# Ten normalisations moved from VectorE to ScalarE in the first of four layers, with the order of work written anew

## The chip, the core and the metric

The kernel runs on one core of a Trainium2 chip. The core has five engines that run side by side, each through its own queue in order: TensorE (PE, with its weight loads shown apart as PEld), VectorE (DVE), ScalarE (ACT), GpSimd (POOL) and SyncE (SP), which issues most of the DMA transfers. The engines wait for each other by semaphores. The metric is the device time of one execution in microseconds (us).

## The reference, cut to what matters

The input x has 2048 rows of 512 in bfloat16. Four layers follow each other, each with a residual: A, B, A, B. Every layer first normalises its rows, without a learned scale.

```python
def _layernorm(x, axis=-1, eps=1e-5):
    m = jnp.mean(x, axis=axis, keepdims=True)
    v = jnp.var(x, axis=axis, keepdims=True)
    return (x - m) / jnp.sqrt(v + eps)

x = x + _A_ref(_layernorm(x, axis=-1), A_wqkv, A_wo)   # linear attention
x = x + _B_ref(_layernorm(x, axis=-1), B_wqkv, B_wo)   # sliding window of 256
x = x + _A_ref(_layernorm(x, axis=-1), A_wqkv, A_wo)
x = x + _B_ref(_layernorm(x, axis=-1), B_wqkv, B_wo)
```

Layer A has 32 heads of 16. It makes q, k and v, applies phi(t) = t + 1 for t > 0 and exp(t) otherwise (plus 1e-6) to q and k, sums k times v and k over all rows, and each q row reads these sums: o = (phi(q) kv) / (phi(q) z). Layer B is softmax attention with the same heads, where a row sees itself and the 255 rows before it. Both end with a multiplication by wo.

## The kernel before, in words

The 2048 rows are 16 tiles of 128 rows, on the 128 partitions. x stays in SBUF (`xres`) and is updated in place by every layer; weights are loaded once.

The class `Plan` writes every piece of work as an operation with a name, the engines that may run it, what it reads and writes, and its PSUM banks. `Graph.add` makes the dependencies. The order is not found at run time: `place` (lines 88 to 120) unpacks a byte table, `TABLE`, that holds the order of all operations, the engine of each (for those that have a choice) and the PSUM bank of each tile. `synchronise` (line 123) turns dependencies into semaphore waits, and `play` (line 912) emits each engine's queue in the table's order. So each engine works strictly in the table's order, and an instruction that waits holds up all that is behind it on its engine. `FILL` (line 857, read at line 945) lists after which of PE's first operations how many matmuls without use are put in. They, and nine more before the first operation (line 921), only keep PE at work until data is there.

Normalisation of a tile is the function `norm` (lines 326 to 335): DVE makes the row statistics (`stats`, L330, and `aggr`, L331, which leaves mean and variance in `mv`), POOL adds the small constant (`eps`, L332, into `ve`) and raises to the power of minus one half (`pow`, L333, into `rs`), and DVE applies it, (x - mean) * rs (`xn`, L334). Then the tile is transposed (`transpose`, line 337). In the first layer PE transposes tiles 0 to 4 (L346) and ACT or DVE copies the result out of PSUM (`Te`, L353); tiles 5 to 15 go by a DMA transpose that SP issues (L340).

The first layer's front half is `layer_a_keys` (lines 428 to 471). For each tile t it normalises, makes k on PE (L369), takes phi of it and multiplies the normalised tile with phi(k) into four PSUM banks that run on over all tiles (operations `g`, two a tile, L444). q (L383) is made for each tile too, two halves a tile. phi (line 388) is three instructions: exp on ACT (`E`, L392), min and add on DVE (`E1`, L393), and a max on DVE (`phi`, L394). After tile 15 the four banks go to SBUF (`ge`, L358), are multiplied by wv (`gv`, L458), and `barrier` (line 473) forms the sums, M = kv wo and the denominators. From then on `middle` (line 733) runs layer A's output, layer B tile by tile and the next layer's front in one pipeline, twice. In it the exponentials of scores (L609, L641), masks (`mk`, L615; `mf`, for the far edge of the window, L649 on POOL or L650 on DVE), and evictions from PSUM (`bqe`, `bke`, `bve`, `ve`: queries, keys and values) share DVE, ACT and POOL.

Loads: SP issues all first loads in the order of line 261, and from the eighth on each waits for an earlier one. The last of the first burst is 1 MB of B's weights (`pb<-in_B_wqkv`), and the DMA transposes of the first layer follow it in SP's queue. While the first layer runs POOL also makes constants and masks and re-orders B's weights (`wBp`, L316).

Of the kernel before, what the change touches and what calls it, by code (L numbers as in the profile page):

```python
# [8 lines left out]
ACT = mybir.ActivationFunctionType  # L9
# [203 lines left out]
class Plan:  # L213
# [112 lines left out]
    def norm(self, t, key, xn_slot, out, wr, by_pe):  # L326

        K = self
        xn, name = (lambda: K.vA[:, t, :], ("vA", t)) if xn_slot is None else (lambda: K.xn[:, xn_slot, :], ("xn", xn_slot))
        self.on("DVE", "stats", lambda e: e.bn_stats(K.stats[:, t, :], K.xres[:, t, :]), key, dve(512), rd=[("xres", t)], wr=[("stats", t)])  # L330
        self.on("DVE", "aggr", lambda e: e.bn_aggr(K.mv[:, t, :], K.stats[:, t, :]), key + 0.01, (66, 150), rd=[("stats", t)], wr=[("mv", t)])  # L331
        self.on("POOL", "eps", lambda e: e.tensor_scalar(K.ve[:, t, :], K.mv[:, t, 1:2], LN_EPS, None, op0=ALU.add), key + 0.02, (300, 330), rd=[("mv", t)], wr=[("ve", t)])  # L332
        self.pow = self.on("POOL", "pow", lambda e: e.tensor_tensor(K.rs[:, t, :], K.ve[:, t, :], K.negh[:], ALU.pow), key + 0.03, (640, 690), rd=[("ve", t), ("negh",)], wr=[("rs", t)])  # L333
        self.on("DVE", "xn", lambda e: e.tensor_scalar(xn(), K.xres[:, t, :], K.mv[:, t, 0:1], K.rs[:, t, :], op0=ALU.subtract, op1=ALU.mult), key + 0.04, dve(512, "ptr"), rd=[("xres", t), ("mv", t), ("rs", t)], wr=[name])  # L334
        self.transpose("T", xn, out, [name], wr, key + 0.05, by_pe)
# [92 lines left out]
    def layer_a_keys(self, ph, base):  # L428
# [5 lines left out]
        for t in range(T):  # L434
            k = 100 * ph + t
            self.norm(t, k - 0.5, None, lambda t=t: K.XQ[:, :, t * P:(t + 1) * P], [("XQ", t)], t < self.par["pe_first1"])
# [359 lines left out]
    r"c-rk(1Jq?nlFo<>WR`8)wr$(CZQHhO+qP|2wQYCpd+)ER>6z)7?d|Q|b9PU~|G&KV2EL5=B3_<%jfrF;8#GZ(6a&T@Hqi{3=q9BR6T`$bsZ44U",  # L796
    r"%cL=}O&pWf#5L)Rnmi_+NpJF+_@=$dVDg##CZkDUI+#JGqse3{nyIFk>0}C+X(qENXq-uCN}435kntv|8Emqc#wMKEX_}bCX1SSenwo4TndxkX",
    r"m>Fh;X=b{ZT_(IaZL*uLCWk3yikrgbuIXlSn&zgv*=_EbnI@6xVa}LbW|qlnhMJY;7gNr(Fsn>YGt8VdtIcq8-?TKn%tvO88DYws(xxPwGb7C?",
    r"6B&w_*=CO!ZO)rH=2w&4d~7b52d0l1W9FK@rnebuJ~1!NJ~PjJYSx;EX1-ZxN|<q`j7bXX%_FnGj5h{0n9s~YlMFVRYUXou(PW29X1^(GqQGU7",
    r"!W=N0%@vaz4w_OB6|S1crZhY;Dd3O+Xbgu<4TG@BJT*tmQIis)!58M4Nd>u0eRJJBHx*13^QCEJu9+9+D^tmof#_i2YZC)<Kuz<FA!uzFaza^n",  # L800
    r"$FwoIpd1J^fp1M)lN(ZlLLHL_(m*>?*QAB-jDrZKDWrqSCOyQ2dL|b1HMLD_=x5?Ud8lRjo48N`JWPa&kQWA+d=MWhK~Xc%#Do0M$Yg{JP#Gqe",
    r"MP{)n01Zq*SYir6LsJ+gnn`A<X$F&EnW+jbpbFH5de9MS!(_9?R5w#h9jI!ynodw3wwVUd5E{XD(;1GL=FkOpn3m8Ux<M;w3+<pQw1(rR4RnAT",
    r"=7i}1lVJ*UhovwTmcdDL2ByKg<}56SZE({}hf`(-yl1w<Ot@uMz${n^=U_Ihg73|0m;*bYC%kVKz#7;IYhfWAhudZm?1Emf8&1F;SPXOFB-}Cc",
    r"Afo9FKbXBRAI?J`*attFjnEG^!8-WBEP<cQX1D--;Ua{CQ*a4BH0vQ8{%peIWe5-b;R;m12rvK+!3H=C5g`I@fk$uzDq<vf0!Lv#RKf#r8XiML",
    r"{1C3fRyYVB!$)uzjzJ`>jFIskM8Rut1*771xDTH~G`xzR!&A5cpFkD73D@v5cnDST8C1htFbN;P3#g8h@eX_e@o@@1hZL9quVX5Vj_*JXjDZO;",
    r"B__d`*bozAGQ5F}a4O!0FJT}w#-un62f@4W6*R@^7z<}$226yhF*e@BjF=p6;d_t?;$SAs4DZ8COoLy;Ec^hnKwA6;vfyAyhjlP3WX1IO6V%0Q",
    r"P!qFZW^9J_uogDK7ML9uV{Kf5&G9yN!ljr4?_g)li7oMG$c0_-7s!pRups^lv#~YK!I$t9+u&UM7M`KOt{4vizlXbs_#ETnJ^T(VcEkHP4+(qV",
    r"4=^7KVO#8udGJRljP)@eR)Zqg0INe@EQ;;0J=TB)xB_cJ0w{((u{f^64p;ygYk}ZO?1%}W1S+n<)z}O3<610<z0qMQT!#;^5B9}Gum#uSVBCO-",
    r"VJmLKB(M=ZF2jeo376w$e1t<_JC??wPzIyfvKZYChY?T?ci=E60y{B=9fIX?DDJ|dFbs>qhZxh=wjbectYc%@;TYTQ!H+SH9f8GRFV?jq@mm~)",
    r"`*4AcYrn@55YH~O`|&%hXWzx-_9%XW@8Kdl8sEo$xY$0mi*Skk0Y}18`wrH(&ujxb3I<?*Y-q<|3LD>kfXi%3`y~#<WB4^bw}bFFCa_=O2|R#}",  # L810
    r"?5B7TM?+(~+<t?fVM2QdGuY4ZG5&}zY({$+U*Jjn2{YLz_ywl1@7SMlEWT?O;xCxij>98pZF74HGu!ca8gtn9Y&zS*PQcW5BA&sVHkD0p6WRA|",
    r"V%yT@vU%)T%wm(+y!ISswfSsEo6R<{*=;AA+cvfNE!k$av+ZixcC!Vn*e<raJ&$TH;IG)jUc`bnnSF_uu#LTpZLP6|th0S>Ve4%>8_t%r8*P6J",
    r"c9ZRA2U@i4ZFt+$4zerk0K3`tvV-k5o7DEUrR;V)#73~CZ6CYCma)6+P}{+lwY%*a`++TIciOeKyxn6f*dlhF9cGK#y>_J?ZY$bi_K+Q6E7?`{",
    r"h>d7V*wr?Y9cK^QG4Q1=ZpT7o`<2~lCqOFt+HSF_X*{&D<KURBY+KtX_JmDCRcusS)sD2s?T5CSU2m(~kL(6J+NP!Pc7jbuAKRlgJ)N@??I@dp",
    r"+EWM0NEhrR`-#m&pW2i5yxnIf+p%_vooe^nj`W%R$zHNw*aP;IJ!pTno#?dv#eQec*ex{8cBb#`S-X|G(69Eg%}rzMHu}NlAxn8F8%?)NUFk=g",
    r"ox0IWOLWoZpl__wb~4nR9POaYw3C25Wg(<p^tlx(Kw0UE{ni$ut2P|Xum$OwooS2Ebvw(3r=oPj&bBvg1e#-S*<w_IBGNY$i3(Fi>P^L|58bwv",
    r"s0`h)ed${&OC{(#ia{l*GL@t6X(;ue;gpZcQ&0MVO3{y$pLSCf8b&`+Y3fB)X(UynyS6%wrV(_{)}@~*CXJ$46q)YZ*ffB0QWSb%2hu}(l=e_m",
    r"8brq^4o#)wRF4MJ7@9_LDH_G2TvVSP+4wY_hENT9Y!gsTicSe>u5Cc`Y%MxK4XHmJr1`cEO{9L*hz`+Mnnb_Q6FZI?(+rwSP3RPjr@b_RPSX@h",
    r"MEmFrC8qs!j*?JQnn`Er0yU$gG>ekadAdcj3HT(<q1%Lfkrq*H61IGYu95Nyx<Sq9E;(*N*Xa^nrj~S*!gDKHOjjr(U!^6~nj&yyUP||98Aav$",
    r"w4Czs3W~xHXeGtwhm@Zq@pFp9tLRrMz%MB-&!yF5I62Luc$|WwaU1eHpHfnMK0<9N0WYMpe3;tNIZnur=mjkx=Ew97CE{?rhTf$ow3dk9qxX3o",  # L820
    r"CFc(~I<Kdc{60OS4RoGUa18!{I&n<?kUr$%9E(5V#9We}(#M>HOK@RM%}Kc+cjjbVgwyaf?!wo(D3{{${1I)W3j8q@<4shWEAnP4!-Y5%-{8tz",
    r"mM?H6uFB>3BH!dHe2IJWE$+kB_!GL#pHg4$&T08G>c>6#bNYnS@fXyCKjrjXoj>Cm+>0~taPG?e`Ewr0HTer3z#}*#*Wye(m<MtL&dguZARfx2",
    r"_$$i7mw5<(O<8#<U*Y9k!w%zRT${V`3a)9davdJcb$JXo<gr}KHsXa`pU3fH9?xI$B5ustxE^QcCY*ztGRQ`5#$WMf&dJSr32$PQuek-U<=p%Y",
    r"uj7`yh4b)w{+1_jUf#eHITugj?|3VJ&y#r@ujC*2N1no~cq(t_X}p75@oH|*cX&Fl;TilB-{pI}ldUwD`@D-E@NVA2E#x8Z<<|U&_i-DZ$1}MD",
    r"&*#UypWE^QCOOE5cow(g!#tax@DYB>3z+37pW<UYhv)KfKF!a#BR}U8e3D=A8GeV~<@fk!ZYFspkNm>L<X0{t;ib4lkfQRE3rPtv5>Z47O96=_",
    r"`6RNGl>DMnN(zdT($Z2|Nf~J^V`ZGglr~aUdP^T^E90e|#FF;XSC&W==^*{2qb!w9;w7r|mkBaJVoNs}D9fa~Oq9+tNG3@S2`7VPvUHK2GDPA?",
    r"Ihi6|rI!qqxDri<NqLzn!)1g_laW$EmP<t$CDCQNtdJ_QQpU(CsVp;OmduvXGE*wae5oo6WR9$sW3o{0$Xq!gG32f+lC5%F?#VpaCEMh_ES5bI",
    r"MYqcuiK@Hhft-?u5=}plM{-)CYZ)!8XC#K6lusq5K9&z9mX^~e@|k=t@g%m!m-3oecF0GvRuV`Yt)Tm4uT<1^@`db|N}5nM$a>i+N#uZ>m8bHt",
    r"B$8*6R1V5Uc`lb^lN^#{a#*fNa@i~|<Q+L8Tja7Fl`rL8`9$LCR}xRJ%KLIouE}|cuV2fLazPU4Mfq7OYf`-~-$*k3NfK&uttN@|S4pYW#b_1%",
    r"R=$(8@{7Ebbn?BtCpDz5{vhcEG?k{%dYVB}Yeu;tH>JL&QPEq1npjoSs@1AW>NK6QR@3mBUTdh=>RMAXXf~~-Q#FT9(~KHUhv;<8u8nl4HqlI)",  # L830
    r"Q-^70ZLGsJmqySmnny=yR*k45b(E%%+!{$!%4jX5sU)wC(d?31a!6!NBl)z57S`IDUz=)9X{H6Vffm(F(n1?*X2~T5^|mC@+|pdzX&oJ_?X`op",
# [182 lines left out]
```

## Time and profile before

| | us |
|---|---|
| median of 8 runs (lowest, highest) | 431.86 (430.44, 432.97) |
| the profiled execution | 431.93 |
| its span, first to last instruction | 430.2 |
| PE busy (share of the span) | 392.8 (91%) |
| DVE busy | 355.7 (83%) |
| ACT busy | 347.7 (81%) |
| POOL busy | 127.9 (30%) |

How to read it: the page gives one execution. A line such as "L334 DVE TENSOR_SCALAR vp<-xres,mv,rs" names the source line, the engine, the operation and the tensors written and read; "x14" is a count. In a timeline the first number is the start in us from the beginning of the span and the second the duration; several instructions in a row can be one line. What stands in brackets is the time the engine was idle just before, and what ended that idleness. Matmuls are pipelined, so their ends are modelled, and a matmul's duration is longer than the pace at which they follow each other. In a table by stretches each engine has its busy time and, in brackets, its instructions. The granted clock is the share of full speed at which TensorE was allowed to run. `vp` is the tensor that holds the normalised tiles of the first layer in its first half and phi(k) in its second.

### The profile page before, as it was taken

The page shows a single profiled execution, that of the slowest core. Times are in us where ns is not written, and L with a number is a line of the kernel's source. Part 1 is how long each engine was busy: PE and PEld are TensorE (multiplying, and loading weights), DVE is VectorE, ACT ScalarE, POOL GpSimd, SP SyncE. Part 2 cuts the span into 40 slices and gives each one's busy share as a digit, 9 for nine tenths or more (in the row PEclk, how much of TensorE's full clock was granted, in tenths as well). Part 3 has the DMA queues.
Part 4 walks back from the last instruction along what each step waited for, and adds up shares of the span by engine and source line. Part 5 has one row for each costly group of instructions (what it writes and reads, how often), then busy time and mean ns, then how long its engine had stood idle before and what let it go on. Part 6 is the DMA issues. An engine that isn't in the chain of part 4 may idle for free.

```text
span 430.2 us, 17035 instructions
## 1 busy us (share of the span) xinstructions
PE 392.8 (91%) x7471; PEld 258.0 (60%) x7548; DVE 355.7 (83%) x796; ACT 347.7 (81%) x433; POOL 127.9 (30%) x223
## 2 busy tenths in 40 slices
PE   8799999998899999999999999999798979998775
PEld 3445676766465566565566768576556746665544
DVE  5998899998998799898887789988797688866464
ACT  2433547998999999999997255999998989999992
POOL 4789222101240242121302303213044324242000
PEclk9999999999999999999999999999999989999889
DMA  7933015442152533552323001461443522553321
GB/s 240 274 74 87 2 33 168 116 101 65 39 124 51 108 98 74 113 99 67 81 46 56 15 2 50 110 119 42 113 76 89 117 77 68 106 136 99 79 53 50
DMA packets 66978, 37.81 MB, mean 88 GB/s; under 512 B 48248, under 2 KB 61816, under 8 KB 66904
## 3 DMA queue, kind: packets, MB, share of 16 engines
q1 hardware_dynamic: 66176, 34.75, 35.1%
q0 software_dynamic: 720, 1.97, 1.3%
q8 instruction: 59, 0.97, 1.0%
q14 instruction: 15, 0.12, 0.1%
q10 hardware_dynamic: 8, 0.00, 0.0%
HBM read 6.29 MB, written 2.10 MB: 20 GB/s over the span
## 4 chain that ended last, share of the span: by engine, by line
PE 40%; ACT 38%; DVE 14%; issue 4%; DMA 2%; POOL 1%; SPq 0%; POOLq 0%; ACTq 0%
ACT pb L609 24%; PE ps L369 14%; PE ps L383 11%; ACT pb L641 7%; PE ps L674 6%; PE ps L599 4%; ACT vp L609 4%; DVE vp L394 2%; DVE XQ L526 2%; DVE stats L330 2%; ACT tE L392 2%; DVE tE L393 1%; DMA xres<-in_A_x_dram 1%; DMA XQ<-vp 1%; DVE vp L334 1%
## 5 line engine op out<-in xcount | busy, mean ns | idle before, releaser
L609 ACT ACTIVATE pb<-ps 128x1024 bf16<-128x1024 f32 (+2 forms) x224 | 207.7, 1036 | 7.8 <-PE ps L599 6.7
L674 PEld LDWEIGHTS ps<-vB,pb 128*128 128x128 bf16 x2560 | 78.1, 96 | 13.3 <-DVE pb L615 2.9
L674 PE MATMUL ps<-vB,pb 128*128 128x34 bf16 x2560 | 83.8, 178 | 2.0 <-DVE pb L615 0.6
L392 ACT ACTIVATE tE<-ps 128x512 bf16<-128x512 f32 x64 | 39.0, 613 | 40.9 <-PE ps L369 18.7
L383 PE MATMUL ps<-xT,wBp 128*128 128x128 bf16 x1024 | 69.6, 220 | 2.3 <-DVE pb L650 1.5
L332 POOL TENSOR_SCALAR ve<-mv 128x1 f32<-128x1 f32 x64 | 16.5, 258 | 175.6 <-DVE mv L331 173.8
L383 PEld LDWEIGHTS ps<-xT,wBp 128*128 128x128 bf16 x1024 | 58.9, 98 | 14.9 <-issue 3.8
L615 DVE TENSOR_TENSOR pb<-pb,tri 128x512 bf16<-128x512 bf16 x112 | 47.7, 433 | 11.9 <-ACT pb L609 11.2
L599 PE MATMUL ps<-XQ,kB 32*128 32x256 bf16 (+2 forms) x1024 | 50.3, 271 | 6.8 <-ACT pb L609 3.7
L641 ACT ACTIVATE pb<-ps 128x1024 bf16<-128x1024 f32 x50 | 49.7, 1071 | 1.4 <-PE ps L632 1.4
L369 PE MATMUL ps<-wA,XQ 128*128 128x512 bf16 x177 | 46.2, 380 | 4.0 <-DVE vp L394 0.7
L537 DVE TENSOR_TENSOR xres<-ps,xres 128x512 bf16<-128x512 f32 x63 | 43.0, 684 | 8.3 <-PE ps L369 7.3
L649 POOL TENSOR_SCALAR_AFFINE_SELECT pb<-pb 128x1024 bf16<-128x1024 bf16 x30 | 35.2, 1174 | 38.1 <-ACT pb L641 36.9
L330 DVE BATCH_NORM_STATS2 stats<-xres 128x6 f32<-128x512 bf16 x64 | 43.1, 680 | 3.0 <-DMA xres<-in_A_x_dram 2.4
L333 POOL TENSOR_TENSOR rs<-ve,negh 128x1 f32<-128x1 f32 x64 | 37.1, 579 | 5.3
L383 PE MATMUL ps<-XQ,wA 128*128 128x128 bf16 x512 | 36.1, 219 | 0.4 <-DVE vp L394 0.2
L369 PE MATMUL ps<-M,XQ 128*128 128x512 bf16 x115 | 32.4, 387 | 4.0 <-ACT vp L609 1.2
L599 PEld LDWEIGHTS ps<-XQ,kB 32*128 32x128 bf16 x1024 | 15.4, 93 | 34.1 <-ACT pb L609 15.1
L383 PEld LDWEIGHTS ps<-XQ,wA 128*128 128x128 bf16 x512 | 30.6, 98 | 7.6 <-DVE vp L394 1.2
L369 PE MATMUL ps<-wBv,xT 128*128 128x512 bf16 x106 | 31.1, 385 | 2.7 <-issue 0.8
L369 PE MATMUL ps<-wBo,oT 128*128 128x512 bf16 x104 | 29.4, 387 | 4.5 <-DVE vp L555 1.2
L685 DVE RECIPROCAL rc<-ps 128x16 f32<-128x16 f32 x64 | 16.1, 251 | 16.3 <-PE ps L674 15.8
(109 smaller groups left out, 540.6 us busy)
## 6 DMA issues: line engine op xcount, KB each, us to landing
vB<-vS SPq DMA_DIRECT2D x64, 136.0 KB, 2.6
kB<-vp SPq DMA_DIRECT2D x64, 128.0 KB, 2.2
out_dram<-xres POOLq DMA_DIRECT2D x15, 128.0 KB, 2.7
wA<-in_A_wqkv_dram SPq DMA_DIRECT2D x3, 512.0 KB, 6.3
xres<-in_A_x_dram SPq DMA_DIRECT2D x2, 512.0 KB, 5.0
pb<-in_B_wqkv_dram SPq DMA_DIRECT2D x1, 1024.0 KB, 8.9
xres<-in_A_x_dram SPq DMA_DIRECT2D x3, 256.0 KB, 5.3
wAo<-in_A_wo_dram SPq DMA_DIRECT2D x1, 512.0 KB, 7.6
```

The source lines that it names most:

```text
L330: self.on("DVE", "stats", lambda e: e.bn_stats(K.stats[:, t, :], K.xres[:, t, :]), key, dve(512), rd=[("xres", t)], wr=[("stats", t)])
L333: self.pow = self.on("POOL", "pow", lambda e: e.tensor_tensor(K.rs[:, t, :], K.ve[:, t, :], K.negh[:], ALU.pow), key + 0.03, (640, 690), r ...
L369: m = e.matmul(K.ps(ps), lhs(c), rhs(c), start=c == 0, stop=c == 3)
L383: m = e.matmul(K.ps(ps)[:, f * P:(f + 1) * P], w(c, f), xT(c), start=c == 0, stop=c == 3)
L392: self.on("ACT", "E", lambda e: e.activation(K.tE[:, s, :], K.ps(ps), ACT.Exp, bias=0.0), key, act(512), wr=[("tE", s)], ps=[ps])
L537: self.on("DVE", "res", lambda e: e.tensor_tensor(K.xres[:, t, :], K.ps(po), K.xres[:, t, :], ALU.add), key, dve(512), rd=[("xres", t)], w ...
L599: m = e.matmul(K.ps(ps[gq])[:, ns * i:ns * i + ns], K.kB[rows, j % 4, 2 * f + b, :, :], K.XQ[rows, f, q:q + ns], start=True, stop=True, ti ...
L609: return e.activation(out(2 * h, 2, ns), i, ACT.Exp, bias=0.0, scale=0.25)
L615: return e.tensor_tensor(x, x, K.tri[:, 0, :].unsqueeze(1).unsqueeze(1).to_broadcast([P, 4, n, 64]), ALU.mult)
L641: return e.activation(far(h), i, ACT.Exp, bias=0.0, scale=0.25)
L649: return e.affine_select(out=x, in_=x, compare_op=ALU.is_ge, fill=0.0, base=-2, pattern=[[0, 16], [-2, 64]], channel_multiplier=1)
L674: m = e.matmul(K.ps(ps)[:, 34 * u:34 * u + 34], K.P((b // 2) % rp)[:, gq, f, o:o + P], K.vB[:, (b // 2) % 4, b % 2, r, :], start=i == 0, s ...
```

## The change: what it does

In the first layer, for tiles 2 to 11, `xn` is no longer one DVE instruction (x - mean) * rs but an ACT instruction, Identity(rs * x + b), with one scale and one bias per row. The bias b = -mean * rs is a new operation, `nb`, which may run on POOL or DVE and writes over `ve`. Tiles 0, 1 and 12 to 15 of the first layer and all later layers keep `xn` on DVE. Besides, `eps` may now run on DVE in all layers.

```diff
-        self.on("POOL", "eps", lambda e: e.tensor_scalar(K.ve[:, t, :], K.mv[:, t, 1:2], LN_EPS, None, op0=ALU.add), key + 0.02, (300, 330), rd=[("mv", t)], wr=[("ve", t)])
+        small = {"POOL": (300, 330), "DVE": (66, 150)}
+        self.g.add("eps", small, lambda e, eng: e.tensor_scalar(K.ve[:, t, :], K.mv[:, t, 1:2], LN_EPS, None, op0=ALU.add), key + 0.02, rd=[("mv", t)], wr=[("ve", t)])
         self.pow = self.on("POOL", "pow", lambda e: e.tensor_tensor(K.rs[:, t, :], K.ve[:, t, :], K.negh[:], ALU.pow), key + 0.03, (640, 690), rd=[("ve", t), ("negh",)], wr=[("rs", t)])
-        self.on("DVE", "xn", lambda e: e.tensor_scalar(xn(), K.xres[:, t, :], K.mv[:, t, 0:1], K.rs[:, t, :], op0=ALU.subtract, op1=ALU.mult), ...
+        if by_act:
+            self.g.add("nb", small, lambda e, eng: e.tensor_scalar(K.ve[:, t, :], K.mv[:, t, 0:1], K.rs[:, t, :], -1.0, op0=ALU.mult, op1=ALU.mult), key + 0.03, rd=[("mv", t), ("rs", t)], wr=[("ve", t)])
+            self.on("ACT", "xn", lambda e: e.activation(xn(), K.xres[:, t, :], ACT.Identity, bias=K.ve[:, t, :], scale=K.rs[:, t, :]), key + 0.04, act(512), rd=[("xres", t), ("ve", t), ("rs", t)], wr=[name])
+        else:
+            self.on("DVE", "xn", ...
...
-            self.norm(t, k - 0.5, None, ..., [("XQ", t)], t < self.par["pe_first1"])
+            self.norm(t, k - 0.5, None, ..., [("XQ", t)], t < self.par["pe_first1"], 2 <= t < 12)
...
-FILL, SPARE = {1: 2, 4: 1, 6: 6}, 6
+FILL, SPARE = {1: 1, 6: 5, 7: 1}, 6
```

`TABLE` is replaced as a whole. Unpacked, the two tables compare so:

- Operations: PE 858 in both, SP 228 in both, DVE 795 before and 827 after, ACT 432 and 443, POOL 219 and 186.
- `eps` is on DVE for 13 of the first layer's 16 tiles and for 19 of the 48 later ones. Nine of the ten `nb` are on DVE, that of tile 7 on POOL.
- Later engine choices: 12 `mf` go from POOL to DVE and 10 from DVE to POOL. `bve` 1, 3 and 11 and `bqe` 10 and 13 go from DVE to ACT, `bke` 11 and `bve` 12 from ACT to DVE, all in the second layer; `ve` 9 and 14 go to DVE at its end. One `ge`, one `bke` and one `Te` go to DVE; one `oTe`, one `recb` and one `Te` go to ACT.
- Order: of PE's 858 operations 248 stand elsewhere among the others, by at most 12 places; SP's first 27 are as before. In the first layer the transpose of tile 3 now stands ahead of the k of tile 2, and one more `g` stands ahead of the k of tile 5. ACT's queue begins Te 1, E 0, E 2, xn 2, xn 3, Te 2, Te 3, E 4, xn 5, xn 4, E 6, Te 4, xn 6, E 3, E 8, xn 8.

## The prediction

> **What bounds the kernel now.** The time per stretch comes first, because the change works in the first 60 us of a 430 us span. The columns are the stretch, its length, and the busy time of PE, weight loads, DVE, ACT and POOL, then the granted clock, the DMA share and GB/s.
>
> ```profile
> 12.00:25.00 13.00, 10.78 (x64) 4.76 (x64) 12.95 (x35) 5.26 (x9) 9.90 (x24) 1.00 0.85 227
> 25.00:37.00 12.00, 11.78 (x94) 6.03 (x94) 11.37 (x26) 3.47 (x6) 10.61 (x19) 1.00 0.33 67
> 37.00:43.00 6.00, 5.64 (x52) 3.08 (x53) 4.57 (x9) 2.84 (x5) 5.49 (x9) 1.00 0.47 110
> 43.00:54.00 11.00, 10.50 (x158) 7.45 (x159) 9.79 (x18) 6.03 (x12) 3.10 (x5) 1.00 0.01 1
> ```
>
> From 12 to 25 us DVE never rests (12.95 of 13.00) and ACT is 40% busy: there is room to move work to ACT. PE is idle for 2.2 us there, but for only 0.2 of the next 12. So DVE is late early, and from 25 us on PE is the bound. A gain can only be PE's lost slots, and the timeline of PE alone shows those that are marked:
>
> ```profile
> 14.02 0.40 PE L346 MATMUL ps<-ident,vp 128*128 128x128 bf16 x4 [0.27 <-DVE vp L334]
> ...
> 18.02 0.40 PE L346 MATMUL ps<-ident,vp 128*128 128x128 bf16 x4 [0.30 <-DVE vp L334]
> ...
> 19.59 1.02 PE L369 MATMUL ps<-wA,XQ 128*128 128x512 bf16 x4 [0.74 <-DVE vp L394]
> 21.34 1.04 PE L369 MATMUL ps<-wA,XQ 128*128 128x512 bf16 x3 [0.74 <-DMA XQ<-vp]
> ...
> 39.29 1.07 PE L383 MATMUL ps<-XQ,wA 128*128 128x128 bf16 x16 [0.21 <-DVE vp L394]
> ```
>
> Two waits are for xn of tiles 3 and 4 (L334, what the change moves), one for a phi (L394, queued behind xn on DVE), and one for the first DMA transpose, tile 5. Each costs about 0.17 more than marked, since the last matmul's modelled end (0.38 for 512 columns, while eight in a row take 1.89, so 0.216 each) hides the drain. Together: 0.44 + 0.47 + 0.91 + 0.91 = 2.73 up to 21.34, and 0.38 at 39.29.
>
> Then the DMA answers, for that fourth wait:
>
> ```profile
> pb<-in_B_wqkv_dram SPq DMA_DIRECT2D x1, 1024.0 KB, 8.9
> XQ<-vp SPq DMA_TRANSPOSE x11, 2.5
> DMA to landing us min/median/max: 2.4/2.5/4.7
> ```
>
> The last weight load of the burst is issued at 11.89 and takes 8.9, so it lands at 20.8. Tile 5's transpose, issued at 16.61, needs 4.7 where the usual one needs 2.5, and lands at 21.3, half a us after that load. It stood behind the load.
>
> **The change part by part.** Durations are those of the profiled execution: 430.2 span, 431.93 in all, so 1.73 outside it; it stands 0.07 above the median of the eight runs, 431.86.
>
> xn off DVE. These rows give the prices:
>
> ```profile
> 24.98 0.41 DVE L334 TENSOR_SCALAR vp<-xres,mv,rs 128x512 bf16<-128x512 bf16 x1
> 25.31 0.17 DVE L331 BATCH_NORM_AGGREGATE mv<-stats 128x2 f32<-128x6 f32 x1
> 25.40 0.66 DVE L394 SCALAR_TENSOR_TENSOR vp<-ps,tE 128x512 bf16<-128x512 f32 x1
> 14.45 0.60 ACT L353 ACTIVATE XQ<-ps 128x512 bf16<-128x512 bf16 x1 [0.44 <-PE ps L346]
> ```
>
> The ten xn of tiles 2 to 11 are the third to the twelfth of their row: 0.40, 0.64, 0.38, 1.28 for two, 0.39, 0.40, 0.41, 0.41 and 0.41, in all 4.72; less the 0.09 by which the next one overlaps each, DVE gets back 3.8.
>
> Onto DVE in layer one: nine of the ten biases and 13 of the 16 eps, by the new table. No row has that form on DVE; aggregate (L331) is the nearest in size, 0.09 from start to start and 0.17 alone. The bounds are 22 x 0.09 = 2.0 and 22 x 0.17 = 3.7. I take 2.2, because the new order puts other work between most dependent pairs. DVE nets 1.6 (between 0.1 and 1.8).
>
> On ACT: ten of 0.60 by the copy of equal size (L353); the dearest 128x512 eviction, L554, is 0.77. That is 6.0 to 7.7, beside 5.26 of 13 busy and 3.47 of the next 12: cover that is there. Each xn adds a wait to ACT's queue (bias, scale), and behind it stand the evictions Te and exps E, which DVE's E1 and PE's next bank wait for. Walking the new queue, xn 3 ends near 11.8 (13.96 before), xn 5 near 14.7 (16.6), xn 4 near 15.5 (18.0). Te 2 falls behind xn 3: near 12.3 against 11.8, so tile 2's k starts some 0.3 later; tile 3's transpose, now ahead of it, no longer stops PE afterwards.
>
> [...]
>
> A second function on ACT beside Exp and Copy: the trace has one table load (1.28 at 2.02) for 433 instructions of two kinds. If Identity needed another, up to 18 switches of 1.28, 23 us; taken as zero, because Copy already shares Exp's.
>
> PE, the sum. The first three waits (1.82) go. What is late next is tile 5's transpose: SP would issue it near 14.7 instead of 16.61, but it still stands behind the load that lands at 20.8. So PE's fourth wait grows from 0.9 to nearly 2. Tile 5's k starts near 20.9 (0.44 earlier) with one more g group (0.43) done ahead of it by the new PE order: 0.87 at that point. From there PE streamed to the end of the stage but for 0.25 near 35.2, 0.38 at 39.29 and 0.22 near 41.0; DVE now runs over 1 us ahead, so I take 0.7 of these 0.85. Stage: -1.55, bounds -0.3 (fourth wait only, all else taken by dearer small instructions) and -2.7 (every marked wait up to 21.34).
>
> POOL loses 13 x 0.258 here and gains one bias; its 9.9 of 13 busy falls, and wBp, which it makes by 40 us, is wanted at 59.7: worth nothing. FILL goes from nine warming matmuls to seven, in gaps where PE waits for tile 2 (10.73): nothing, unless the granted clock, which is full in all these stretches, falls late; if it came after k 0 and k 1 they would take 1.7 longer, of which the gap before tile 2 hides 0.5: at most 1.2.
>
> Later layers. DVE gets 19 eps at 0.09 to 0.17 (1.7 to 3.2), and two more far masks on balance (12 from POOL, 10 to it) at 0.71 (L650): 1.4. DVE is 0.6 to 0.95 busy there and ACT up to 0.99, so DVE's queue hides most. ACT takes five evictions between 65 and 190 us and gives two, then gives two at the second layer's end: near zero over all, plus or minus 1.8 where they lie. The other orders differ by swaps of neighbours: of PE's 858 items 248 shift, none by over 12. I charge 0.25 for all of this; a gain from swaps is as possible as a loss, bounds -1 and +2.
>
> Sum: -0.87 - 0.7 + 0.25 = -1.3. Against 431.93 that is 430.6.
>
> **The rivals.** *Same:* the transpose wait is all that matters early. DVE's saving is used up by the 22 small instructions at 0.17 (net 0.1), the later waits stay, and only 0.44 is won, less 0.25: 431.7. For it: DVE stays the fullest engine. Against: three of the four waits are for things queued behind xn.
>
> *Larger gain:* the transpose lands early too. For it: the load is nearly through by 18.5. Then all 2.73, and 0.85 later, less the charge 0.25, is 3.3; with the two ends half met, 2.5: 429.4. Against: the landing half a us after the load.
>
> *Slower:* ACT in layer two. Five evictions come to it (bve 1, 3 and 11, bqe 10 and 13: three of 0.675 by L358 into vS and two of 0.605 by L358 into XQ, 3.2), two leave (bke 11, bve 12: 0.77 + 0.675). Net +1.8 between 65 and 190 us, where ACT is 78 to 98% busy; with a stage gain of only 0.3: 433.4. It decides once ACT's loss there exceeds the stage's gain, that is, if ACT paces PE already from 65 us, not only from 110. For it: 19.45 and 19.61 of 20 busy at 110 and 150 us. Against: bve 1 and 3 lie at 65 to 86, where ACT still has gaps, and leave +0.44 behind them.
>
> *Not what it says:* Identity reloads tables, 431.9 + 23 = 455.
>
> **How the numbers follow.** Main 0.46, same 0.19, larger 0.14, slower 0.19, reload 0.02. About 0.2% (0.86 us) is what a measurement of this kernel can tell from none, so faster is below 431.0 and slower above 432.7. The main case's own range is 429.9 to 431.3; five sixths of it is below 431.0. Faster: 0.39 + 0.14 = 0.53. Same: 0.07 + 0.19 = 0.26. Slower: 0.21. The range reaches from the larger case's 429.0 to the slower one's 433.4.
>
> **What would show it.** DVE under 12.5 of 13 in 12 to 25 us and ACT over 9; xn rows on ACT of 0.6 to 0.8; no PE wait for L334 at tiles 3 and 4; a PE wait of over 1 us for the DMA at 20 to 21; the first score matmuls 1 to 1.5 us earlier. It is wrong if tile 5's transpose lands before 20, if Te and E stand behind xn so that PE starves before 20 us, if a second table load appears, or if the lead won by 60 us is gone by 200.

## The result, and the profile after

| | before | after |
|---|---|---|
| median, us (lowest, highest) | 431.27 (429.95, 434.06), 32 runs | 434.8 (433.23, 438.08), 11 runs |
| ratio after / before | | 1.0091, 95% interval 1.0070 to 1.0113 |
| profiled execution, span | 431.93, 430.2 | 434.8, 433.1 |
| last product of the first layer's stage (first `gv`) starts | 49.51 | 51.75 |
| the rest, from there to the end of the span | 380.7 | 381.35 |

The changed kernel is slower by 3.5 us, where 1.3 less had been forecast. Line numbers of the changed file are five higher from `xn` on: `xn` on ACT is L337, on DVE L339, the DMA transpose L345, k L374, scores L604.

The table by stretches of the changed kernel, with the columns of the one shown before (PE, weight loads, DVE, ACT, POOL, granted clock, DMA share, GB/s):

```profile
12.00:25.00 13.00, 9.96 (x73) 5.21 (x73) 9.78 (x36) 8.57 (x15) 9.10 (x19) 0.94 1.08 218
25.00:37.00 12.00, 11.92 (x85) 6.00 (x86) 10.82 (x30) 5.63 (x9) 7.13 (x13) 0.93 0.28 55
```

DVE is no longer full from 12 to 25 us (9.78, was 12.95), as the change meant. But PE did less there too (9.96, was 10.78), and its clock was not full in either stretch. PE's own timeline of the changed kernel says why; in brackets stands the idle time before and what ended it:

```profile
11.74 0.40 PE L351 MATMUL ps<-ident,vp 128*128 128x128 bf16 x4 [0.31 <-ACT vp L337]
...
18.43 1.90 PE L449 MATMUL ps<-vp 128*128 128x512 bf16 x8
23.12 1.69 PE L374 MATMUL ps<-wA,XQ 128*128 128x512 bf16 x4 [2.79 <-DMA XQ<-vp]
25.02 1.49 PE L449 MATMUL ps<-vp 128*128 128x512 bf16 x3 [0.22 <-issue]
```

The waits for xn of tiles 3 and 4 are gone, and one large wait has taken their place: PE is through with its work at 20.33 and stands 2.79 us for the DMA transpose of tile 5. The matmuls behind it are slow: four of 512 columns take 1.69 where four in a row took 1.03 before. The clock record of the trace has half speed from 23.36 to 26.77, one piece of 3.41 us. SyncE's timeline of the changed kernel, and the summary of the first layer's transposes in it, show the transpose itself:

```profile
11.29 0.37 SPq L259 DMA_DIRECT2D pb<-in_B_wqkv_dram  x1
15.69 8.14 SPq L345 DMA_TRANSPOSE XQ<-vp  x4
...
DMA to landing us min/median/max: 2.4/2.5/7.4
```

Tile 5's transpose was issued 0.92 earlier than before (16.61) and landed 1.77 later (23.07 against 21.30): 7.4 us where it had taken 4.7. Each transfer has 16 landing marks in the trace. The 1 MB load landed at 20.02 to 20.17, so no later than before (its last part came at 20.79 there), fifteen parts of the transpose at 21.92 to 22.03, the last at 23.07. Before, the transpose had landed 0.51 behind the load; here it is 2.90.

ScalarE's timeline of the changed kernel:

```profile
10.39 0.60 ACT L397 ACTIVATE tE<-ps 128x512 bf16<-128x512 f32 x1 [0.61 <-PE ps L374]
10.88 1.60 ACT L337 ACTIVATE vp<-xres,ve,rs 128x512 bf16<-128x512 bf16 x2
...
17.35 0.80 ACT L337 ACTIVATE vp<-xres,ve,rs 128x512 bf16<-128x512 bf16 x1
```

An xn on ACT is 0.80, ten of them 7.9 in the table of groups, and there is still one table load in the whole run (1.28 at 2.02).

Three later waits stand out on PE's timeline of the changed kernel; at the first of these places PE did not wait before, at the other two it waited 0.6:

```profile
69.39 0.40 PE L604 MATMUL ps<-XQ,kB 32*128 32x256 bf16 x8 [0.99 <-DVE xn L339]
...
398.71 0.55 PE L604 MATMUL ps<-XQ,kB 32*128 32x256 bf16 x8 [1.46 <-DVE o L691]
...
418.92 0.29 PE L604 MATMUL ps<-XQ,kB 32*128 32x128 bf16 x8 [1.58 <-DVE o L691]
```

All are scores (L604). The first is the first block of scores of layer two; the other two wait for the division that writes `o`. The same three blocks on PE's timeline of the kernel before:

```profile
68.37 0.40 PE L599 MATMUL ps<-XQ,kB 32*128 32x256 bf16 x8
...
396.29 0.40 PE L599 MATMUL ps<-XQ,kB 32*128 32x256 bf16 x8 [0.61 <-ACT pb L609]
...
415.63 0.29 PE L599 MATMUL ps<-XQ,kB 32*128 32x128 bf16 x8 [0.56 <-DVE o L686]
```

To see where time is won and lost over the whole span, each weight load of PE (the n-th of its source line) was compared with the same one in the profile of before. The table gives the median lateness in us in stretches of before's time, for the changed kernel and for six of the runs told below:

| stretch | 40-55 | 70-85 | 265-280 | 340-355 | 385-400 | 415-430 |
|---|---|---|---|---|---|---|
| the changed kernel | 2.24 | 2.63 | 3.47 | 1.51 | 1.75 | 2.57 |
| first layer changed only (e5) | 0.79 | 1.07 | 1.03 | -1.22 | -0.38 | -0.49 |
| later order changed only (e6) | -0.32 | 0.46 | 0.39 | -1.57 | -0.93 | 0.18 |
| changed, end as before (e14) | 1.61 | 2.15 | 2.74 | 0.78 | 0.66 | 0.27 |
| changed, two repairs (e13) | -1.78 | -1.80 | -1.62 | -3.26 | -4.05 | -2.75 |
| changed, three repairs (e15) | -2.10 | -1.37 | -1.17 | -3.09 | -3.20 | -2.40 |
| before, two repairs (e16) | 0.50 | 0.51 | 0.81 | -0.81 | 0.03 | -0.07 |

Every row falls by 1.6 to 2.3 between 280 and 340 us, also the one with before's order (e16): that is the one execution of before that was profiled, which has two waits of 1.52 and 1.20 at 306 and 326 us that the others have not, or only in part. It must not be counted as a gain of any run. The rest reads plainly. The first layer costs 2.2 in the changed kernel's profile. Between 55 and 85 us 0.4 more goes in it and 0.8 in e6. From 385 us to the end the rows with the new order lose 0.8 to 1.3 (the changed kernel, e6, e13); of those with the old order e5, e14 and e16 lose nothing, and e15 loses 0.8, for which no cause was shown.

### The profile page after: what moved, and what is told of

It reads as the page before. It is cut to its first block, busy times and chain, and to the rows that moved or that the text cites. A ratio compares the mean times of both kernels' runs of the same rounds, so it can differ in the third digit from the quotient of the medians.

```text
span 433.1 us, 17049 instructions
## 1 busy us (share of the span) xinstructions
PE 394.7 (91%) x7469; PEld 259.2 (60%) x7546; DVE 356.2 (82%) x828; ACT 354.4 (82%) x444; POOL 119.0 (27%) x190
## 4 chain that ended last, share of the span: by engine, by line
PE 52%; ACT 24%; DVE 15%; DMA 5%; issue 2%; POOL 0%; SPq 0%; ACTq 0%
PE ps L374 19%; ACT pb L614 16%; PE ps L388 12%; PE ps L679 9%; PE ps L604 5%; ACT pb L646 4%; DVE XQ L531 3%; PE ps L449 3%; DVE xres L542 2%; DMA XQ<-vp 2%; DVE stats L330 2%; ACT vp L614 1%; DVE XQ L399 1%; DMA xT<-xn 1%; ACT tE L397 1%
## 5 line engine op out<-in xcount | busy, mean ns | idle before, releaser
L614 ACT ACTIVATE pb<-ps 128x1024 bf16<-128x1024 f32 (+2 forms) x224 | 207.4, 1030 | 11.5 <-PE ps L604 10.7
L620 DVE TENSOR_TENSOR pb<-pb,tri 128x512 bf16<-128x512 bf16 x112 | 47.6, 430 | 13.0 <-ACT pb L614 12.2
L604 PE MATMUL ps<-XQ,kB 32*128 32x256 bf16 (+2 forms) x1024 | 50.3, 271 | 8.8 <-DVE o L691 3.0
L374 PE MATMUL ps<-wA,XQ 128*128 128x512 bf16 x177 | 47.7, 393 | 5.0 <-DMA XQ<-vp 2.8
L604 PEld LDWEIGHTS ps<-XQ,kB 32*128 32x128 bf16 x1024 | 15.3, 93 | 38.5 <-ACT pb L614 14.4
L374 PE MATMUL ps<-wBv,xT 128*128 128x512 bf16 x107 | 32.8, 397 | 2.9 <-issue 1.3
L333 POOL TENSOR_SCALAR ve<-mv 128x1 f32<-128x1 f32 x32 | 7.8, 244 | 97.0 <-DVE mv L331 96.6
L374 PE MATMUL ps<-M,XQ 128*128 128x512 bf16 x113 | 30.7, 380 | 3.6 <-DVE XQ L531 1.8
L374 PE MATMUL ps<-wBo,oT 128*128 128x512 bf16 x105 | 29.9, 387 | 4.4 <-ACT pb L614 0.7
L374 PEld LDWEIGHTS ps<-wA,XQ 128*128 128x128 bf16 x192 | 17.1, 100 | 23.6 <-issue 3.5
```

The source lines that it names most:

```text
L374: m = e.matmul(K.ps(ps), lhs(c), rhs(c), start=c == 0, stop=c == 3)
L604: m = e.matmul(K.ps(ps[gq])[:, ns * i:ns * i + ns], K.kB[rows, j % 4, 2 * f + b, :, :], K.XQ[rows, f, q:q + ns], start=True, stop=True, ti ...
L614: return e.activation(out(2 * h, 2, ns), i, ACT.Exp, bias=0.0, scale=0.25)
L620: return e.tensor_tensor(x, x, K.tri[:, 0, :].unsqueeze(1).unsqueeze(1).to_broadcast([P, 4, n, 64]), ALU.mult)
```

## The experiments

Three theories stood at the start: A, the loss is in the first layer (the transpose of tile 5 and the half clock behind PE's wait for it); B, ScalarE's dearer xn and their place in its queue delay the first layer; C, it is the new order of the later layers. "Ratio" is against the kernel before, run beside it on the same chip, with its 95% interval.

### Which part costs: e4, e3, e5, e6

e4 is the changed kernel with all xn on VectorE again:

```diff
-            self.norm(t, ..., t < self.par["pe_first1"], 2 <= t < 12)
+            self.norm(t, ..., t < self.par["pe_first1"])
```

> Edit: the changed kernel's order everywhere, but xn of tiles 2 to 11 is again one VectorE instruction, at the same place in the order, and the bias is left out; eps stays where the new order has it. Theory A: DVE reaches tile 5's xn near 15 to 16, so its transpose is issued at about the same time as in the changed kernel or 0.5 later; if it lands past 22 again, PE's wait and the half clock return and the time is 433.5 to 436; if it lands at 21 to 21.5 the time is 431 to 433. Theory B: the time is that of the kernel before, within 1. Theory C: 434 to 435, whatever tile 5 does.

Measured: 434.3 (431.56 to 440.24), ratio 1.0072 (1.0042 to 1.0102). The first `gv` was at 49.62, as in the kernel before; the rest took 382.8. Most of the loss is there without any xn on ACT, and in this profile, in which tile 5's transpose took 6.4 from its issue at 14.47 and its k started at 20.94, it all lies behind the first `gv`. That is more than e6 below shows for the later order alone (1.0036), but the intervals of the two overlap.

e3 is the reverse: the order of the kernel before, with xn of tiles 2 to 11 on ACT at the place that they had on DVE, the bias on DVE and eps on POOL.

> Edit: the kernel before with its own order everywhere; only xn of tiles 2 to 11 goes to ScalarE, with its bias on VectorE, both at the place where xn stood; eps stays on GpSimd. Theory A: tile 5's xn ends about where it did, so its transpose lands at about 21.3, PE's waits are those of before, and the time is 430.3 to 432 (within 1 of the kernel before). Theory B: ScalarE delays E and Te, PE waits more for L369's neighbours in 12 to 30 us, and the time is 2 to 4 slower than before. Theory C: as fast as before or a little faster, since the later order is that of before.

Measured: 433.74 (432.03 to 435.3), ratio 1.0040 (1.0007 to 1.0073); `gv` at 51.34, the rest 380.56. Here PE waits for xn of tiles 2, 3 and 4, each of them on ACT, as its timeline shows:

```profile
11.22 0.40 PE L351 MATMUL ps<-ident,vp 128*128 128x128 bf16 x4 [0.70 <-ACT vp L337]
15.26 0.40 PE L351 MATMUL ps<-ident,vp 128*128 128x128 bf16 x4 [1.01 <-ACT vp L337]
19.73 0.40 PE L351 MATMUL ps<-ident,vp 128*128 128x128 bf16 x4 [1.03 <-ACT vp L337]
```

So in the order of before theory B holds: the new order of the first layer is needed to hide the dearer xn. That order issues tile 5's transpose earlier.

e5 and e6 cut the order in two behind the last `gv`: e5 has the changed first layer and before's order for the rest, e6 before's first layer (xn on DVE) and the changed order for the rest.

```diff
 e5:  operations 1 to 325 as changed (with xn on ACT)
-     the rest as changed
+     the rest as before
 e6:  operations 1 to 315 as before (xn on DVE, no bias)
-     the rest as before
+     the rest as changed
```

> The first 325 operations in the changed kernel's order, with the normalisation on ScalarE; from the last gv on, every engine's order is that of the kernel before (PE: 97 instructions as changed, 771 as before). If the loss sits in the first layer (theory A: tile 5's transpose, and the clock that falls in its wait), gv stays near 51.7 and the time is 433.5 to 435. If the new order of the later layers costs it (theory C), gv may stay late, but the rest from gv to the end is back at 380.7 or under, and the time is 431 to 433. If both, half of each: near 433.

> The mirror image: the first 315 operations in the order of the kernel before, xn on VectorE and no bias, and after them the changed kernel's order. Theory A: the time of the kernel before, 431 to 432, with the rest after gv at 380.7. Theory C: 433 to 434.5, with the rest 1.5 to 3 longer.

Measured: e5 433.95 (430.37 to 436.82), ratio 1.0063 (1.0035 to 1.0090); e6 432.77 (430.1 to 436.14), ratio 1.0036 (1.0011 to 1.0060). Neither A nor C has it alone: +0.63% for the first layer, +0.36% for the later order, together 0.99% against 0.91% measured for both. (The execution of e5 that was profiled, 431.48, lies near the lowest of its times.)

### The transpose of tile 5: e1, e2, e7, e8

e1 moves the 1 MB load behind four transposes in SyncE's queue of the changed kernel; e2 leaves the load where it was and puts ten matmuls without use in front of PE's wait, to keep its clock.

```diff
 e1, SP queue:
-... wAo  wBn  T5 T6 T8 T7  T9 ...
+... wAo  T5 T6 T8 T7  wBn  T9 ...
 e2, PE's queue, ahead of the wait for tile 5's DMA:
+    for _ in range(10):
+        e.matmul(self.PS[:, o.tiles[0].banks[0], :], warm[:, 0:P], warm, start=True, stop=True)
```

> Edit: the changed kernel, but the 1 MB load of B's weights stands behind the transposes of tiles 5, 6, 8 and 7 in SP's queue instead of ahead of them. Theory A (the early transposes run into the weight load, tile 5 lands late, PE stands still for 3 us and its clock falls to half): tile 5 lands 2.4 to 3 us after its issue, PE's 2.8 us wait at 23.1 is gone, no half-speed piece at 23 us, and the time falls by 3 to 5 us, to 430 to 432. Theory B (ScalarE: ten instructions of 0.80 and their place in ACT's queue delay the first layer): the time stays within 1 us of the changed kernel's 434.8. Theory C (the later layers' new order costs it): likewise no change beyond 1 us.

> Edit: the changed kernel with ten useless 512-column matmuls in front of the wait for tile 5's transpose, written to the PSUM bank that the next product overwrites. Theory A says the wait has two parts, the idle time (2.97) and then 3.4 us at half clock, which cost about 1.9 in work that took twice as long: with PE kept at work the clock stays at 1.0 after 23 us and the time falls by 1.5 to 2.2, the wait itself staying. Theories B and C: the same time within 0.5, since PE waits for others anyway. A third view, that the half clock costs nothing because DVE paces the stage there, also expects no change.

Measured: e1 432.89 (430.17 to 436.74), ratio 1.0020 (0.9983 to 1.0057); e2 436.63 (435.52 to 437.72), ratio 1.0115 (1.0082 to 1.0149). From PE's timeline of e1:

```profile
20.71 1.04 PE L374 MATMUL ps<-wA,XQ 128*128 128x512 bf16 x4 [1.68 <-DMA XQ<-vp]
```

With the load out of the way tile 5 starts 2.4 earlier than in the changed kernel and the clock stays full there (1.00 from 12 to 25 us); `gv` comes at 49.23. The transpose was still not quick: issued at 14.39, it took 6.3 to land, where the median of the eleven is 2.6. In e2 the clock did not fall at 23 us (the wait left was 2.09, and the four matmuls of 512 columns behind it took 1.04) and `gv` came at 50.02, yet the time did not fall (the intervals of e2, four runs, and of the changed kernel overlap): PE then waited 2.27 at 68.95, and the 24 matmuls of 128 columns from 69.78 took 2.77, where the changed kernel's took 1.50. In this profile the gain in the first layer was lost 20 us later, at the first scores of layer two.

e7 takes the DMA out of it: in the changed kernel PE turns tiles 5 and 6 as well, and VectorE copies the result. e8 is the same with the later order of before.

```diff
-pe_first1=5
+pe_first1=7
 PE:   k9 [T5] g0 g7 [T6] g2 g4 k10        (T5, T6 were on SP)
 DVE:  stats11 [Te5] nb6 eps7 [Te6]
```

> The changed kernel with tiles 5 and 6 of the first layer turned by TensorE (4 more transposes of 128 columns each, 2 copies on VectorE of some 0.4) in place of the DMA. Theory A: the wait of 2.8 at 23 us is gone, k of tile 5 starts near 20.5 to 21, gv at 49.5 or before, no half clock at 23 us; the time falls by 2 to 3, to 431.5 to 432.5. Theory C: the wait goes too, and the time falls by 1 at most, to 433.5 to 434.

> Both at once: the first layer of the changed kernel with tiles 5 and 6 turned by TensorE, and the later layers in the order of before. If both causes are real and add, gv near 49 and the rest 380.7: 430 to 431, level with the kernel before or up to 1 under it. If either is no cause, 432 to 433.5.

Measured: e7 433.44 (431.19 to 435.91), ratio 1.0043 (1.0015 to 1.0071); e8 429.88 (428.5 to 432.97), ratio 0.9982 (0.9959 to 1.0005). One stretch of e7's table:

```profile
12.00:25.00 13.00, 12.31 (x92) 6.71 (x95) 12.12 (x43) 10.52 (x17) 7.87 (x17) 1.00 0.59 191
```

PE is busy 12.31 of 13.00, where it had 9.96, and `gv` comes at 48.74, 3.0 before the changed kernel's. That settles the first layer: its loss is that of the first transposes by DMA (tiles 5 and 6, moved together), and not theory B's, since xn stays on ACT here; the five profiles with these transposes on PE have `gv` at 46.92 to 48.74. But with the later order as changed, 0.8 of the 3.0 is left at the end of the profiled span (e7), while with the order of before the median falls by 4.1 (e8 against e5). The line of PE's timeline of e7 where it goes:

```profile
68.00 0.50 PE L604 MATMUL ps<-XQ,kB 32*128 32x256 bf16 x8 [2.60 <-DVE XQ L399]
```

### The first scores of layer two: e12, e13, e11

The changed table has the first block of scores (`s0`) ahead of `aout9`, `bk4`, `bk5` and `aout10` in PE's queue, behind which it stood before (the first text below names `q23`, which is ahead of it in both). It reads kB, which SyncE stores from the evicted keys (`kd`), and the second of these stores (`kd1`) is issued behind the 512 KB load of wBo. That load is ahead of the store in the order of before too, where the store landed at 67.48 and the scores started at 68.37, without a wait; now they want it sooner. In the eight profiles with this order the scores start at 66.8 to 69.8. In the changed kernel that is 0.24 after the landing of that store (69.15), though xn stands in the brackets; in e2 and e9 the brackets name the store itself, and the longest wait there, in e9 below, has "3.19 <-DMA kB<-vp". e12 and e13 move the load; e13 has PE's transposes of e7 too.

```diff
 SP queue of layer two, e12 and e13:
-T17 kd0 wBo kd1 T18 vd0 T19 ...
+T17 kd0 kd1 T18 vd0 T19 wBo ...
```

> The changed kernel with one load moved in SyncE's queue: wBo (512 KB) behind T18 and T19 instead of ahead of kd1. If the scores of layer two, which the new order put ahead of q23 and aout10, wait at 66.8 to 69.8 for the store of k behind that load (0.99 in the changed kernel's profile, up to 3.19 where PE came earlier), the wait falls under 0.4 and the time by 0.6 to 2: 432.8 to 434.2. If the order of VectorE holds them (the profile names xn), nothing changes: 434.5 to 435.

> The changed kernel with tiles 5 and 6 of the first layer turned by TensorE and the load of wBo moved as in the run beside it. With the transposes alone PE won 3.0 by the last gv and gave back 2.6 in the wait of the scores at 68.0 and about 1.2 in the half clock that followed; if both are the load's doing, 430 to 431.5. If the load has no part, 433.4 again.

Measured: e12 434.69 (433.16 to 436.88), ratio 1.0074 (1.0046 to 1.0103); e13 429.59 (427.91 to 432.85), ratio 0.9955 (0.9930 to 0.9980). In both profiles the wait of `s0` is gone. By itself that is hardly worth anything (the intervals of e12 and of the changed kernel overlap: there PE comes late, and the wait was only 0.99). With the transposes it is worth 3.9: e7 and e12 alone lower the ratio by 0.0048 and 0.0017, both together by 0.0136. The two causes hide each other; whoever removes only one sees little.

Whether the load alone makes the long waits is open. In the changed kernel the store landed 0.42 after the load (68.73), and the scores started 4.25 after its issue at 65.14. In e9 they started 6.46 after its issue at 63.36, and what held the store there was not shown. e12 and e13 put it ahead of the load.

e11 makes the same move in e8, where wBo's load stood right ahead of T18. The one large wait after the first layer in PE's timeline of e8 was for that transpose:

```profile
66.49 1.05 PE L388 MATMUL ps<-xT,wBp 128*128 128x128 bf16 x16 [1.54 <-DMA xT<-xn]
```

```diff
 SP queue of layer two, e11:
-T17 kd0 wBo T18 kd1 vd0 T19 ...
+T17 kd0 T18 kd1 vd0 T19 wBo ...
```

> The changed first layer, tiles 5 and 6 turned by TensorE, the later order of before, and the 512 KB load of wBo issued behind the second layer's transposes T18 and T19. In the run without this last edit PE waited 1.54 at 66.49 for T18, issued right behind that load. If the load holds it, the wait falls under 0.5 and the time to 428.6 to 429.3. If the transposes are held by what else is in flight there (stores, code), the time stays at 429.5 to 430.2.

Measured: 429.08 (427.43 to 430.07), ratio 0.9931 (0.9906 to 0.9955). The wait is gone in the profile, and this kernel beats both.

### The last 45 us: e9, e14

VectorE's timeline of the changed kernel around the wait of 1.46 at 398.71:

```profile
395.22 0.25 DVE L690 RECIPROCAL rc<-ps 128x16 f32<-128x16 f32 x1
395.92 0.69 DVE L655 TENSOR_TENSOR vp<-vp,tri 128x1024 bf16<-128x1024 bf16 x1 [0.45 <-ACT vp L646]
396.53 1.35 DVE L620 TENSOR_TENSOR pb<-pb,tri 128x512 bf16<-128x512 bf16 x1
397.81 0.24 DVE L690 RECIPROCAL rc<-ps 128x16 f32<-128x16 f32 x1
397.98 0.68 DVE L691 TENSOR_TENSOR o<-ps,rc 128x256 bf16<-128x256 f32 x2
```

A far mask that was on POOL (`mf50`, L655) and a mask (L620) stand between the reciprocal and the divisions that free PE's banks. Around the wait of 1.58 at 418.92 it is a mask (`mk123`, which itself waits for ACT) ahead of the reciprocal, and a far mask (`mf55`) between it and the division (`div60`):

```profile
416.93 0.42 DVE L620 TENSOR_TENSOR pb<-pb,tri 128x512 bf16<-128x512 bf16 x1 [1.50 <-ACT pb L614]
417.27 0.25 DVE L690 RECIPROCAL rc<-ps 128x16 f32<-128x16 f32 x1
417.84 0.69 DVE L655 TENSOR_TENSOR pb<-pb,tri 128x1024 bf16<-128x1024 bf16 x1 [0.32 <-ACT pb L646]
418.45 0.41 DVE L691 TENSOR_TENSOR o<-ps,rc 128x256 bf16<-128x256 f32 x1
```

e9 moves two other divisions up:

```diff
 DVE queue, e9:
-rcp54 mf50 mk112 rcp55 div54 div55      rcp58 mk121 div58
+rcp54 div54 mf50 mk112 rcp55 div55      rcp58 div58 mk121
```

> The changed kernel; on VectorE only div54 and div58 (the division that writes o and frees a bank of ps) are put back right behind their reciprocals, ahead of mf50 with mk112 and of mk121. If the two waits of the scores on o near the end (1.46 and 1.58) come from these two places, they fall to the 0.6 each of before, and the time by 1 to 2: 432.8 to 433.8. If ScalarE's exponentials hold the scores there anyway, as they did before, the waits change their name only: 434.3 to 435.

Measured: 435.92 (433.74 to 439.35), ratio 1.0116 (1.0071 to 1.0161). The edit missed its target: the first wait is still there (1.31 at 400.40), since PE waits for div55, which stayed behind mf50 and mk112; the second was for div60, which was not moved. Its profile also has the wait of 3.19 named above, and slow matmuls behind it: two of 512 columns took 1.06 at 72.55, where the next two took 0.60. e14 therefore puts the whole end back:

```diff
 operations 1 to 2300 of 2542 as changed
-the rest (from about 380 us) as changed
+the rest as before, mf50 on POOL
```

> The changed kernel up to operation 2300 of 2542 (some 380 us), and from there every engine in the order of the kernel before, mf50 back on GpSimd. If the new order of the last 45 us costs what the profiles show (1.3 to 2.2 from 385 us on, with two waits of 1.5 on o), the time falls by 1 to 2: 432.8 to 433.8. If the clock does it there and not the order, 434.5 to 435.

Measured: 433.55 (431.07 to 438.19), ratio 1.0050 (1.0022 to 1.0078). The two waits in e14's timeline of PE:

```profile
396.95 0.40 PE L604 MATMUL ps<-XQ,kB 32*128 32x256 bf16 x8 [0.61 <-ACT pb L614]
...
416.52 0.29 PE L604 MATMUL ps<-XQ,kB 32*128 32x128 bf16 x8 [0.56 <-DVE o L691]
```

The first is the 0.61 that before had at this place, the second its 0.56, and the lateness does not grow any more after 385 us. So the end of the new order costs 1.2 by the medians, 1.8 by the ratios; but the interval overlaps that of the changed kernel, so the two waits are shown and their price is not clear of noise.

### All together, and the control: e15, e10, e16

> The changed kernel with all three repairs: tiles 5 and 6 of the first layer turned by TensorE, wBo's load behind T18 and T19, and the order of before from operation 2300 on. If the three causes are separate and add, the 429.59 of the first two falls by the 1.2 that the last won alone (434.8 to 433.55): 428.0 to 428.9. If the end is set by something the first two already removed, 429.3 to 430.

e15 has the edits of e7, e12 and e14. Measured: 428.09 (427.08 to 429.57), ratio 0.9927 (0.9909 to 0.9946). With e11 it is the fastest of the study: 3.0 under the kernel before, and 1.6% under the changed one by the two ratios. The three gains were forecast as separate; the step from e13 to e15 is 0.28%, with intervals that overlap. One stretch of e15's table:

```profile
12.00:25.00 13.00, 12.45 (x82) 6.00 (x79) 12.40 (x45) 9.97 (x17) 9.15 (x19) 1.00 0.68 219
```

PE and DVE are near full in the stretch that the change was made for, and ACT is at 9.97, where it had 5.26 before the change.

e10 and e16 ask whether that is the change's doing or only the repairs'. Both are the kernel before with tile 5 turned by PE; e16 also has wBo's load later.

```diff
-pe_first1=5
+pe_first1=6
 PE:   g5 [T5] k8 k9 k10
 ACT:  Te4 [Te5] E8
 SP, e16 only:
-T17 kd0 wBo T18 kd1 vd0 T19
+T17 kd0 T18 kd1 vd0 T19 wBo
```

> The kernel before with its one late transpose, that of tile 5, on TensorE (one copy of 0.6 on ScalarE), the normalisation left on VectorE. If the gain of the run with the changed first layer, two transposes on TensorE and the later order of before (429.88) is that of the transposes, 429.5 to 430.3. If ScalarE's normalisation has its part in it, only the wait of 0.74 at 21.3 goes, less 0.4 of transposes: 430.8 to 431.6.

> The kernel before with the two repairs that are not the change's: tile 5 turned by TensorE and the load of wBo behind T18 and T19; the normalisation stays on VectorE, and the whole order is that of before. If the 2.5 of the run with the changed first layer and the same repairs (429.08 against 431.59) came from the repairs alone, 429 to 429.8. If ScalarE's normalisation in the first layer has its part, the wait of 0.93 on the store of k at 69.5 goes and little more: 430.6 to 431.6.

Measured: e10 431.92 (429.85 to 433.63), ratio 1.0014 (0.9992 to 1.0035); e16 430.78 (429.98 to 432.41), ratio 0.9979 (0.9954 to 1.0004). e16's table by stretches:

```profile
12.00:25.00 13.00, 11.19 (x73) 5.24 (x73) 13.00 (x33) 5.89 (x11) 9.90 (x24) 1.00 0.70 227
```

DVE is full there, and PE cannot use what the transpose gave. The repairs without the change are worth 0.2%, and the interval reaches to none; with the changed first layer they are worth 0.7%. So the changed first layer, in which tile 6 too is turned by PE, is worth some 2 us (e11 against e16, ratios 0.9931 and 0.9979, run on different chips, with intervals that just touch), and three things hid it. What tile 6 on PE has of these 2 us was not tried apart.

## Why the prediction was wrong, step by step

- **DVE is full and late, and moving xn frees it.** Right: 9.78 for 12.95, and no wait for xn at tiles 3 and 4. With the first transposes out of the way DVE's relief is a gain (e11 and e15 against e16).
- **An xn on ACT is 0.60 to 0.77.** Low: 0.80. The copy that gave 0.60 reads no scale and no bias for each row, as an xn does; whether these two make the 0.20 was not tried. The ten cost 7.9 on ACT, 0.2 more than the upper bound; in the changed order PE waits for one only at tile 2 (0.31 at 11.74).
- **No second table.** Right, one load, of 1.28. **ACT over 9 in 12 to 25 us.** Missed at 8.57, since PE starved; 9.97 in e15.
- **"So PE's fourth wait grows from 0.9 to nearly 2" and "Tile 5's k starts near 20.9".** This is the step that failed. The mechanism was named and its size was not: the wait grew to 2.79 and k started at 23.12, 2.2 later than forecast. The forecast let the transpose land as soon as the load has (20.8, then k at 20.9), though even in the one profile at hand it was 0.51 behind it. In the changed kernel the load landed at 20.17, which is earlier than the 20.8 assumed, but the transpose 2.90 behind it: fifteen parts 1.86 behind, the last another 1.04. In the nine profiles in which PE waits for this transpose with the load ahead of it, tile 5's k starts 4.7 after the issue with the first layer's order of before (before, e6), and 6.4 to 8.9 after it with the new order (the changed kernel, e2, e4, e5, e9, e12, e14), at 20.85 to 23.12 in all. Issuing earlier is not by itself later: in e4, issued at 14.47, k starts at 20.94. What holds the transpose is open; in the changed kernel a packet of instruction code ended 0.98 before its last part landed. At the first `gv` the stage stood at +2.24, where -1.55 had been summed, and 2.2 of that miss of 3.8 is this step.
- **The clock, "at most 1.2".** The term was put at the wrong place: at the start, for FILL. There the record starts at full clock at 6.49 before and at 9.71 in the changed kernel, where k 0 and k 1 took 3.12; with the same FILL these eight matmuls took 1.89 to 1.93 in ten other profiles, and 2.97 and 3.25 in e9 and e7, so FILL alone does not set it. What was not priced is the half clock behind the longer wait: after the 2.79, one piece of 3.41 us from 23.36 at a granted 0.5, which can cost up to half its length, 1.7 (an estimate from these two numbers). With the 2.2 above that is about the stage's miss.
- **"I charge 0.25" for the later layers.** Wrong: e6 puts the new order at +0.36%, 1.6 us, inside the bounds of -1 and +2. Its two places are the first scores at 67 to 70 us and the end. The order was judged by how far instructions shift (none by over 12 places) and by the busy shares, and neither shows that a store behind a load is wanted sooner, or a mask that comes between a reciprocal and a division.
- **The rival on the other side, "ACT in layer two".** It gave the right side for a reason that isn't there: from 70 to 280 us the changed kernel loses 0.8 in all, and over the span ACT waits longer ahead of the exponentials for PE's scores (11.5 us in the group's row, 7.8 before): ACT became less of a bound, not more.
- **"If the lead won by 60 us is gone by 200".** That sign was right in kind: in e2, e7 and e9 the lead went at 67 to 70 us.

The chain that ended last, from the page of the changed kernel, shows the same shift:

```profile
PE 52%; ACT 24%; DVE 15%; DMA 5%; issue 2%; POOL 0%; SPq 0%; ACTq 0%
```

Before it was PE 40, ACT 38, DVE 14 and DMA 2: the end now hangs more on PE and on DMA, and less on the exponentials.

## What to carry to other kernels

Before you free an engine, ask which wait ends next and whether its end moves: here the late engine had hidden a DMA transpose behind a burst of loads, and issued 0.92 sooner it landed 1.77 later. Price a transfer's landing from a run in which it is issued at the new time, or give the few transposes that fall into a load burst to PE. When a gain vanishes, look for the next wait down the line that does not move with it (here a store of keys behind a weight load), and remove both before you judge either.

## What the runs showed of the hardware that was not expected

- **A transpose issued behind a load can land late.** With the 1 MB load ahead of it in SP's queue the first transpose took 3.6 us from its issue to its landing (e3, issued at 17.91), 4.7 (before, 16.61), 6.4 (e4, 14.47), 7.4 (the changed kernel, 15.69) and 8.8 (e2, 14.18), where the median of the eleven is 2.5 in each. In e1, with the load behind it, it took 6.3, so the load alone does not explain it. The load itself took 8.9 in the changed kernel as before.
- **A code packet next to a late landing.** In the changed kernel one of the 16 parts of the transpose came 1.04 after the others (23.07 against 22.03), 0.98 after the end of an 8 KB packet of instruction code (20.27 to 22.09). That is one profile, and whether the code's packet causes it was not tried.
- **Half clock behind PE's waits.** In the first 75 us PE's marked waits of 1.54 (e8), 1.68 (e1), 1.80 (e9) and 2.09 (e2) had matmuls at full pace behind them: sixteen of 128 columns took 1.05 in e8, four of 512 took 1.04 in the other three. Behind those of 2.27 (e2), 2.60 (e7), 2.79 (the changed kernel), 2.97 (e5), 3.19 (e9), 3.48 (e14) and 3.86 (e12) they were slow: four of 512 columns took 1.56 to 1.89 (the changed kernel, e5, e12, e14) and 24 of 128 took 2.17 to 2.77 (e2, e7, e9), where 1.03 and 1.50 are usual. In the changed kernel's clock record that is one piece of 3.41 at 0.5; in e12 the mean granted clock was 0.85 from 12 to 25 us and 0.88 from 25 to 37, which makes 6.8 us at 0.5 (an estimate from these two means). In the records of the kernel before and of the changed one every piece at 0.5 is 3.41 long, but for the last at the end of the record, and the pieces start whole multiples of that length apart (23.36 and 354.45 in the changed kernel are 97 apart). Cut by that grid, the two records have 39 stretches at full clock that start between 12 and 80 us: the one in which PE was idle for 2.79 was followed by half clock, and none of the 38 with up to 1.04 was. Later, idle time alone does not separate them: in the kernel before, a stretch with 1.74 (from 303.45) was followed by full clock and one with 1.36 (from 412.68) by half.
